# Two order tables joined at the first MoE matmul, the first units' attention reading whole copies of their keys

## The chip, the cores and the metric

The kernel runs on one core of a Trainium2 chip. The metric is the time of the device in microseconds; three executions of the kernel before give a median of 778.26 us (778.2 to 780.05). The trace is of one execution more, which took 779.34 us. TensorE (PE in the rows) multiplies, VectorE (DVE), ScalarE (ACT) and GpSimd (POOL) do the element-wise work, and SyncE (SP) issues most transfers. Each runs its own queue of instructions in order.

## What is computed

A block-sparse attention over 4 batches, 8 heads, 768 positions of 64 numbers, in blocks of 32, is followed by a MoE-like layer with one gated product.

```python
B, H, S, D = q.shape                      # 4, 8, 768, 64
scores = scale * np.matmul(q, k.transpose(0, 1, 3, 2))
mask = np.abs(blk_i - blk_j) <= 1
mask = mask | (blk_i == 0) | (blk_j == 0) | (blk_i == n_blocks - 1) | (blk_j == n_blocks - 1)
for qb in range(n_blocks):
    for kb in sampled_blocks[qb]:         # three sampled blocks for each block
        mask[qb * 32:(qb + 1) * 32, kb * 32:(kb + 1) * 32] = True
scores = np.where(mask, scores, -1000000000.0)
attn = softmax(scores)
x = (attn @ v).transpose(0, 2, 1, 3).reshape(B * S, H * D)
h = x @ w_in                              # (3072, 512) @ (512, 2048)
g = h * np.clip(h + 3.0, 0.0, 6.0) / 6.0
return g @ w_out                          # (3072, 2048) @ (2048, 512)
```

## The kernel before

**Units, chunks, weights.** A unit is one batch and four blocks of queries (a "quad" each). The string `SEQ` (line 39) gives their order; units 0, 1 and 2 are groups 1, 2 and 3 of batch 0, so blocks 3 to 14. Three units make a chunk of 384 columns, and the layer runs by chunk in 16 steps `m0`, `m1` and so on: `h` (line 657) is twelve matmuls out of one weight tile, `ga` and `gb` apply the gate, `gh` and `gl` split it into a high and a low part, `o` multiplies it with the output weight of three units. Weights `w0` to `w31` are input and output tiles in turn. They come as 64-bit words and are put together by `size`, `sign`, `low` and `bits`, then split by `hi` and `lo`.

**A unit's keys.** A query block attends to eight slots: the three blocks near it, block 0 and block 23 (the ends), and three chosen by a table. For batch 0 all keys are loaded first into `KN`, in three parts of eight blocks (`keys` of the constants, line 325). For units 0 to 2 only the three chosen blocks are copied on the chip, into slots 5 to 7 of a ring of six buffers `KR` (`chosen`, line 394; the block's number is read into registers by `registers`, line 383, sixteen at a time); near and ends are read from `KN` directly. So `keys_of` (line 443) hands out three places, and `s` (line 474) makes three matmuls of 96, 64 and 96 columns for each of four quads, two halves of the partitions and two heads: 48 for half a unit. Later units load their keys from memory into the ring (`keys` of an item, line 399), five blocks at a slot's first use in a batch and three after that, and three more by number; their `s` is one matmul of 256 columns for each, 16 for a half.

**The chain of a unit.** `s` (scores), `r_` (VectorE: bias and minimum), `e` (ScalarE: exponential), `t` (transposes), `c` (copy out of PSUM), `a` (values), `n_` (division), `x` (transposes), `xh` and `xl` (high and low part of the layer's input). `m0 h` needs those of units 0 to 2. Values come by `values` (SP) and, for the chosen blocks, by `gather` (an indirect transfer that GpSimd issues, with the addresses of the tile `rows`).

**The order.** The string `SCORE` (line 43) is an order written out: `u1 s0` is unit 1's first half of scores, `w4 low.d` the weight 4's `low` on VectorE (`a` ScalarE, `p` GpSimd, `s` SyncE). The loop at the end of `fused_kernel` issues the operations in that order, and `Ordered` (line 232, the operations' line in the profile is 242) keeps each engine's in it. What stands earlier in an engine's queue holds up what stands behind it.

Of the kernel before, what the change touches and what calls it, by code (L numbers as in the profile page):

```python
# [49 lines left out]
chosen0.d; u1 s0; u0 e03 e13; u1 gather0.p; u0 d t01; u1 r_00; w4 size; u0 t10; u1 gather2.p; w4 low.d; u1 e00; u0 t11 c01.d c10.a; u1 s1 r_01; u2  # L50
gather2.p; u0 c11.a; w4 sign; u1 e01 r_02; w1 size; u2 gather1.p; w4 bits; u1 t00; u3 q; u1 e02 r_10 c00.a r_03; u2 gather0.p; u1 e10; w5 load5; u1
r_11 e03; u2 chosen3.d; u0 a; u1 e11; u2 gather3.p; u1 r_12; u2 chosen2.a; w1 low.d; u1 r_13 e12; w1 sign; w0 size; u2 s0; u3 gather2.p; u0 n_; u1
e13; u3 keys1; w0 low.a; w1 bits; w2 size; u1 d; u0 x; u2 r_00; w1 hi.p; w2 low.a; u1 t01; u2 r_01; u1 t10; u2 e00; u3 gather0.p; w2 sign; w8 load8;
u1 t11 c01.a; u2 r_02 s1; u1 c10.a; w1 lo.d; w7 load7; u1 c11.a; u2 r_03 e02; w3 low.p; u2 e01; u1 a; u2 r_10; w6 low.p; u2 e03 r_11 e10; u3
gather1.p; w2 bits; u0 xh; u2 e11 r_12; u0 xl; w3 size; w10 load1; u2 t00; u4 gather1.p; u1 n_; u2 e12 t01 c00.a r_13 t10; u4 gather0.p; u2 c01.a; w0
sign; u1 x; u2 e13; w3 sign; u1 xh; u2 t11 d c10.a; u1 xl; u2 c11.a; w0 bits; w6 size; u2 a; w5 size; w3 bits; w9 load0; u3 keys2 gather3.p; w0 hi.a;
w6 sign; w2 hi.a; w0 lo.d; w3 hi.a; u2 n_; w5 low.a; w2 lo.p; w8 low.a; u2 x; w12 load3; w6 bits; w8 size; u2 xh; w3 lo.d; w7 size; u2 xl; w11 load2;
w7 low.a; w8 sign; m0 h; w7 sign; w10 low.a; u3 values2; w8 bits; w10 size; w7 bits; m1 h; w4 hi.a; w10 sign; m0 ga; w4 lo.d; w9 size; u3 values1; m0
gb; w9 low.a sign; m2 h; m0 gh.a; u3 keys0; w5 sign; m1 ga; m0 gl.d; w6 hi.a; m1 gb; m0 o0; w6 lo.d; w8 hi.a; m1 gh.a; w5 bits; m3 h; u3 values3; m2
ga; m1 gl.d; w12 size; m2 gb; w13 load4; w11 low.p; w12 low.a; u3 values0; w11 size; w8 lo.d; m0 o1; w16 load7; m3 ga; w10 bits; m1 o0; m3 gb; w10  # L60
hi.a; m0 o2; u3 keys3; w9 bits; m1 o1; m2 gh.a; w10 lo.d; m4 h; m2 gl.d; w13 size; w11 sign; w13 low.a; w14 load5; w12 sign; u4 q; w17 load8; m1 o2;
w11 bits; m4 ga; w15 load6; w16 size; m5 h; w12 bits; m3 gh.a; m4 gb; w5 hi.p; w7 hi.a; w12 hi.a; w13 sign; u4 keys0; w16 low.a; u3 s0; w5 lo.d; w12
lo.d; m2 o0; w14 low.a; u3 r_00; m3 gl.p; m6 h; w14 size; u3 r_01; u4 values0; w13 bits; u3 e00; w18 load0; u3 e01 r_02; w7 lo.p; m5 ga; u3 r_03 s1
e02; w22 load4; m5 gb; u3 e03; w14 sign; w20 load2; m2 o1; w15 size; u3 r_10; w15 low.p; w17 size; m3 o0; u3 r_11 e10; w14 bits; u4 keys2; m2 o2; u3
e11 r_12; w17 low.p; m3 o1; w14 hi.a; u3 r_13; m4 gh.a; u3 t00; w14 lo.d; w9 hi.a; u3 t01 t10; m4 gl.d; u3 e13; u5 q; m3 o2; u3 c01.a; w9 lo.d; u4
values1; u3 c10.a; m7 h; w21 load3; w15 sign; m6 ga; w16 sign; w11 hi.a; u3 e12; m6 gb; w19 load1; m5 gh.p; u3 c00.a; m4 o0; w16 bits; w18 size; u4
keys3; u3 t11; m5 gl.d; w16 hi.a; m4 o1; w15 bits; m7 ga; u3 c11.a; m4 o2; w16 lo.d; w20 size; m7 gb; u3 a; w11 lo.p; w13 hi.a; w20 low.a; w13 lo.d;
w22 size; m8 h; u4 keys1; u3 d; u4 gather3.p; w19 size; w17 sign; w21 low.a; u3 n_; w18 low.p; w22 low.a; m5 o0; w17 bits; u4 gather2.p; w19 low.a; u5
keys0; u3 x; m6 gh.d; w21 size; m5 o1; w20 sign; u5 gather0.p; u3 xh; m6 gl.d; m5 o2; u3 xl; m8 ga; u5 gather1.p; m6 o0; w20 bits; m7 gh.a; w15 hi.a;
m6 o1; m8 gb; u4 values2; m7 gl.d; u4 values3 s0; w25 load2; w15 lo.d; m6 o2; w18 sign; u5 values1; u4 r_00; m7 o0; m8 gh.a; w18 bits; u4 e00; u5  # L70
keys1; m7 o1; u4 r_01; w17 hi.a; m8 gl.d; u4 e01; m7 o2; u4 r_02; w17 lo.p; w18 hi.a; u4 r_03 t00 e02 s1 e03; w22 sign; w23 load0; u5 values0; u4
c00.a; w18 lo.d; m8 o0; w20 hi.a; u4 r_10; w25 low.p size; u4 t01 r_11; u6 q; m8 o1; u4 e10; w20 lo.d; u4 e11; m9 h; u4 r_12 c01.a; w22 bits; u4 e12;
u5 keys2; u4 r_13; w21 sign; u4 e13 t10; w23 size; w19 sign; m10 h; w22 hi.a; u4 d; w26 load4; u4 c10.a; w19 bits; m9 ga; w22 lo.d; w24 load1; w19
hi.a; u4 t11; m9 gb; m8 o2; m10 ga; w23 low.p; u4 c11.a; m10 gb; m11 h; m9 gh.a; w19 lo.d; m10 gh.a; w23 sign; u5 keys3; m9 gl.d; u4 a; w23 bits; m11
ga; w26 size; w21 bits; w26 low.a; m11 gb; w27 load0; w21 hi.p; m9 o0; u5 values2; u4 n_; w24 size; u5 values3 gather2.p; w24 low.a; w21 lo.d; u4 x;
m9 o1; m10 gl.d; u4 xh; u5 gather3.p; w24 sign; m10 o0; u4 xl; m9 o2; u6 gather2.p keys3; w24 bits; u5 s0; m11 gh.a; w25 sign; w23 hi.a; u6 gather3.p;
m10 o1; m11 gl.d; w24 hi.a; u5 r_00; w27 size; m10 o2; w24 lo.d; u5 e00; w28 load1; u5 r_01; w27 low.p; m12 h; u5 e01 r_02; w23 lo.d; u5 e02 r_03; w25
bits; u5 e03 s1; m12 ga; w26 sign; w29 load2; u6 keys2; m11 o0; m12 gb; w25 hi.p; u5 r_10; m12 gh.a; u5 t00; w25 lo.d; m11 o1; u5 e10 r_11 c00.a; m12
gl.p; m11 o2; w28 size; u5 r_12; u6 values3; w26 bits; u5 e11 t01; u6 values2; m12 o0; u5 e12 r_13; w28 low.p; w26 hi.a; u5 t10; w27 sign; u5 e13; m12
o1; u5 c01.a; w26 lo.d; u5 t11 c10.a; m12 o2; w27 bits; u5 c11.a; m13 h; w29 size; u5 d; w30 load0; w27 hi.a; w28 sign; w27 lo.d; u5 a; w28 bits; m13  # L80
ga; w29 low.d; w28 hi.a; w31 load1; m13 gb; w28 lo.d; u6 s0; m13 gh.a; u8 gather0.p; u6 values4; w30 low.a; u5 n_; m14 h; m13 gl.d; w30 size; u6 r_00;
# [696 lines left out]
```

## Time and profile before

| | us |
|---|---|
| median of three executions | 778.26 |
| lowest, highest | 778.2, 780.05 |
| the profiled execution, whole | 779.34 |
| its span, first to last instruction | 777.6 |
| busy in the span: TensorE | 754.0 |
| VectorE | 520.9 |
| ScalarE | 406.5 |
| GpSimd | 187.3 |
| start of `m0 h` in the span | 58.46 |

The profile gives busy time by engine and by slice, the groups of instructions with their mean time, and instructions in order of time with the idle time ahead of them and what ended it. Times in the rows count from the start of the span. A busy TensorE need not be at its peak, and matmul ends are modelled. The names of tiles are those of the code: `kn` and `kr` are `KN` and the ring, `att`, `h` and `out` are PSUM banks that the first units share.

### The profile page before, as it was taken

How to read it: one execution, taken by the hardware profiler on the slowest of the kernel's cores; microseconds unless marked ns; L12 is line 12 of the kernel's file. 1: busy time of each engine (PE TensorE's matmuls, PEld its weight loads, DVE VectorE, ACT ScalarE, POOL GpSimd, SP SyncE). 2: the span in 40 equal slices, each digit the busy share in tenths (PEclk: the TensorE clock that was granted, in tenths of full speed). 3: DMA queues.
4: the chain of work that ended last, by engine and by line, in shares of the span. 5: the costliest groups of instructions: out<-in, count | busy, mean ns of one | idle time of the engine just before them, and what ended most of it. 6: DMA issues, size and time to landing. Idle time of an engine off the chain costs nothing.

```text
span 777.6 us, 22739 instructions
## 1 busy us (share of the span) xinstructions
PE 754.0 (97%) x9078; PEld 649.8 (84%) x9078; DVE 520.9 (67%) x1304; ACT 406.5 (52%) x996; POOL 187.3 (24%) x200
## 2 busy tenths in 40 slices
PE   5789999999999999999999999999999999999996
PEld 5679887888888888898888888888888898889985
DVE  2568988955565665565656666767777677676763
ACT  2677977847555656455656553343543522452122
POOL 4531434141332221102123004222013511300110
PEclk9999999999999999999999999999999999999999
DMA  9949997660464673147245517464145670201001
GB/s 325 392 171 305 297 301 262 195 211 15 151 184 118 180 234 117 42 122 215 70 143 179 168 43 225 170 185 145 62 148 141 206 255 2 83 3 41 0 1 41
DMA packets 79687, 119.53 MB, mean 154 GB/s; under 512 B 10018, under 2 KB 45990, under 8 KB 79582
## 3 DMA queue, kind: packets, MB, share of 16 engines
q1 hardware_dynamic: 72674, 96.18, 38.6%
q0 software_dynamic: 6640, 21.76, 8.9%
q8 instruction: 72, 1.18, 0.6%
q14 instruction: 33, 0.27, 0.1%
...
HBM read 111.75 MB, written 6.29 MB: 152 GB/s over the span
## 4 chain that ended last, share of the span: by engine, by line
PE 89%; DVE 1%; DMA 0%; issue 0%; ACT 0%; ACTq 0%
PE out L242 35%; PE h L242 33%; PE att L242 21%; DMA out_dram<-ot 0%; DVE wout L242 0%; DVE wlo_in L242 0%; DVE wlo_out L242 0%; ACT ot L242 0%; DVE g L242 0%; DVE win L242 0%; ACTq L242 0%
## 5 line engine op out<-in xcount | busy, mean ns | idle before, releaser
L242 PE MATMUL h<-x,whi_in 128*128 128x384 f32 x1024 | 265.1, 339 | 1.7 <-ACT x L242 1.4
L242 PEld LDWEIGHTS h<-x,whi_in 128*128 128x128 f32 x1024 | 186.9, 189 | 12.3 <-ACT x L242 1.6
L242 PE MATMUL h<-x,wlo_in 128*128 128x384 f32 x512 | 172.9, 338 | 0.3 <-DVE wlo_in L242 0.3
L242 PE MATMUL out<-whi_out,ghi 128*128 128x512 f32 x384 | 162.2, 422 | 0.0
L242 ACT ACTIVATE p<-p,m 128x256 f32<-128x256 f32 x224 | 112.6, 504 | 83.8 <-DVE m L242 82.9
L242 PE MATMUL out<-whi_out,glo 128*128 128x512 f32 x384 | 151.6, 395 | 0.0
L242 PE MATMUL out<-wlo_out,ghi 128*128 128x512 f32 x384 | 151.1, 394 | 0.0
L242 ACT ACTIVATE g<-h,half_b 128x384 f32<-128x384 f32 x128 | 73.0, 580 | 149.2 <-PE h L242 131.6
L242 POOL DMA_INDIRECT vr<-vB,rows x77 | 76.9, 999 | 167.9 <-PE att L242 145.7
L242 DVE SCALAR_TENSOR_TENSOR g<-g,h 128x384 f32<-128x384 f32 x128 | 69.7, 551 | 57.8 <-ACT g L242 57.2
L242 PEld LDWEIGHTS h<-x,wlo_in 128*128 128x128 f32 x512 | 96.5, 188 | 0.6 <-DVE wlo_in L242 0.6
L242 PEld LDWEIGHTS out<-whi_out,ghi 128*128 128x128 f32 x384 | 72.2, 188 | 22.3 <-issue 12.3
L242 DVE TENSOR_TENSOR wlo_out<-wout,whi_out 128x512 fp32r<-128x512 f32 x106 | 76.1, 718 | 21.9 <-ACT whi_out L242 18.9
L242 DVE TENSOR_TENSOR wlo_in<-win,whi_in 128x512 fp32r<-128x512 f32 x107 | 75.2, 704 | 21.0 <-ACT whi_in L242 18.4
L242 DVE CUSTOM_DVE_ANT_1 p<-att,bias 128x256 f32<-128x256 f32 x176 | 68.6, 419 | 25.8 <-PE att L242 25.5
L242 PEld LDWEIGHTS out<-whi_out,glo 128*128 128x128 f32 x384 | 72.1, 188 | 16.3
L242 PEld LDWEIGHTS out<-wlo_out,ghi 128*128 128x128 f32 x384 | 72.5, 189 | 7.7
L242 DVE TENSOR_TENSOR glo<-g,ghi 128x384 fp32r<-128x384 f32 x114 | 67.9, 596 | 14.2 <-ACT ghi L242 12.0
L242 POOL TENSOR_TENSOR wlo_in<-win,whi_in 128x512 fp32r<-128x512 f32 x21 | 27.8, 1322 | 160.1 <-DVE whi_in L242 105.5
L242 ACT CAST ghi<-g 128x384 fp32r<-128x384 f32 x94 | 47.9, 512 | 32.1 <-PE out L242 29.4
L242 ACT COPY pt<-att 128x512 f32<-128x512 f32 x89 | 51.0, 586 | 24.6 <-PE att L242 23.7
L242 PE MATMUL att<-kr,q 64*32 64x256 f32 (+1 forms) x1280 | 59.7, 376 | 0.7 <-issue 0.7
...
## 6 DMA issues: line engine op xcount, KB each, us to landing
...
kr<-kS SPq DMA_DIRECT2D x52, 192.0 KB
vr<-vS SPq DMA_DIRECT2D x49, 192.0 KB
vr<-vS SPq DMA_DIRECT2D x33, 256.0 KB
kr<-kS SPq DMA_DIRECT2D x24, 320.0 KB
kn<-kN SPq DMA_DIRECT2D x12, 512.0 KB
q<-qT SPq DMA_DIRECT2D x24, 256.0 KB
vr<-vB SPq DMA_DIRECT2D x24, 256.0 KB
```

What stands on the lines that cost most here:

```text
L242: self.last = tc.keep_in_program_order(op(*a, **k)).ins
```

## The change

`SCORE` is new up to `m0 h`: 245 operations where there were 206. From `m0 h` on it is the same list of operations in the same order, without three that now stand ahead: `u3 values1`, `u3 keys0`, `w5 sign`. The new part names new operations. `near` copies a block's three near blocks from `KN` into slots 0 to 2, `ends` the two end blocks into slots 3 and 4, for units 0 to 2; all their slots are then in the ring and `s` is 16 matmuls for a half. `ends` runs once for each of the six buffers, and `holds_k` remembers it, so the later loads of these slots fetch three blocks and not five. `numbers` reads three registers for one item ahead of its copies. The small tables come in three loads instead of six, the constants 0.5 and -0.499 are passed as numbers, `warm` runs one exponential early, and `third` loads a part of `KN` (in the order 2, 0, 1).

```diff
-k0 load keys0; u0 q values1 values0 values2 values3; k0 clamp folding number flag; u0 chosen2.a; u1 q; u0 chosen0.p; k0 place; u1 values1 values0; u0
+k0 lp lc third2 lt third0 li third1 warm; u0 q; k0 clamp; u0 numbers2.p numbers1.a numbers3.d numbers0.a; u1 numbers0.a numbers1.p numbers3.d; u2
...
-        def load(self):
+        def lp(self):
             dma.dma_start(out=picked, in_=picks)
-            self.spr = p_tile().rearrange("p i k -> p (i k)")[:NB, :len(GROUPS) * P]
-            for to, src in ((turned, sampled_t), (place, placing), (samp, sampled), (cands, cand), (self.spr, spread), (ident, ident_d)):
-                act.dma_start(out=to, in_=src)
+
+        def lc(self):
+            t = p_tile().rearrange("p i k -> p (i k)")[:NB, :cand.shape[1]]
+            self.samp, self.cands, self.spr = t[:, :NR].bitcast(I32), t[:, NR:NR + 15], t[:, NR + 15:]
+            act.dma_start(out=t.bitcast(I32), in_=cand)
+
+        def lt(self):
+            act.dma_start(out=turning, in_=sampled_t)
+
+        def li(self):
+            act.dma_start(out=ident, in_=ident_d)
...
+        def third(self, i):
+            n = NB // 3
+            dma.dma_start(out=KN[:, n * i:n * (i + 1)].rearrange("p n h k -> p (n h k)"), in_=kN[0, :, n * P * i:n * P * (i + 1)])
+
+        def warm(self):
+            act.activation(out=warm, in_=nobias[:, :1], func=AF.Exp)
...
-            held = self.unit.held
+            o, n, at = 16 * self.unit.g, 16, 4 * self.quad
+            held = self.unit.held if eng is dma else self.held
+            if eng is not dma:
+                o, n, at = o + at, NR, 0
...
+        def near(self, eng):
+            self.has_near = True
+            copy(eng, self.K[:, :3], KN[:, self.blk - 1:self.blk + 2])
+
+        def ends(self, eng):
+            holds_k[self.kn] = self.unit.b
+            copy(eng, self.K[:, 3:5], KN[:, ::NB - 1])
...
-            return [(slice(3 * BLK), KN[rows_, item.blk - 1:item.blk + 2, hp]), (slice(3 * BLK, 5 * BLK), KN[rows_, ::NB - 1, hp]),
-                    (slice(5 * BLK, KEYS), item.K[rows_, 5:, hp])]
+            at, places = 0, []
+            if not item.has_near:
+                at = 3
+                places.append((slice(at * BLK), KN[rows_, item.blk - 1:item.blk + 2, hp]))
+            if holds_k.get(item.kn) != self.b:
+                places.append((slice(at * BLK, 5 * BLK), KN[rows_, ::NB - 1, hp]))
+                at = 5
+            return places + [(slice(at * BLK, KEYS), item.K[rows_, at:, hp])]
...
-                act.activation(out=to, in_=src, func=AF.Identity, scale=2.0 ** -29, bias=low_b)
+                act.activation(out=to, in_=src, func=AF.Identity, scale=2.0 ** -29, bias=LOW)
...
-            act.activation(out=self.g, in_=self.ps, func=AF.Relu, bias=half_b, scale=1.0 / 6.0)
+            act.activation(out=self.g, in_=self.ps, func=AF.Relu, bias=0.5, scale=1.0 / 6.0)
```

TensorE's queue at its start, before (`h` and `att` are the two PSUM banks of unit 0's first scores, `flags` and `place` belong to the tables):

```order
L242 MATMUL att<-turned_f,place 128x24
L242 MATMUL out_269<-flags,p 128x8 x6
L242 MATMUL h<-kn,q 32x96
L242 MATMUL h<-kn,q 32x64
L242 MATMUL h<-kr_73,q 32x96
L242 MATMUL att<-kn,q 32x96
L242 MATMUL att<-kn,q 32x64
L242 MATMUL att<-kr_73,q 32x96
```

and the same place after the change:

```order
L244 MATMUL att<-flags,p 128x8 x6
L244 MATMUL out_257<-turned_f,turned 128x24
L244 MATMUL h<-kr_73,q 32x256
L244 MATMUL att<-kr_73,q 32x256
L244 MATMUL h<-kr_74,q 32x256
L244 MATMUL att<-kr_74,q 32x256
```

Three pieces of a quad have become one, out of the ring alone, and the two small products ahead have changed places. The whole queue has 4352 entries where it had 4544.

ScalarE's queue from the last table loads to its first key copies, before (an entry ISA works out an address, `kr_75` is the buffer of unit 0's third item):

```order
L242 DMA samp<-sampled 24x3
L242 DMA cands<-cand 24x15
L242 DMA p<-spread 24x768
L242 DMA ident<-ident 128x128
L389 TENSOR_LOAD picked
L242 ISA
L242 ACT_TABLE_LOAD
L242 COPY kr_75<-kn 128x128
```

and after (128x256 is `ends`, 128x384 is `near`):

```order
L244 DMA p<-cand 24x786
L244 DMA turned<-sampled_t 4x152
L244 DMA ident<-ident 128x128
L244 ACT_TABLE_LOAD
L244 ACTIVATE warm<-nobias 128x1
L405 TENSOR_LOAD picked x5
L244 COPY kr_76<-kn 128x256
L244 COPY kr_73<-kn 128x384
L244 COPY kr_74<-kn 128x256
```

The copies that need no register now stand ahead of those that do, and the table load ahead of the wait for the keys.

GpSimd's queue at the end of unit 0's gathers, before (`vr_` is a buffer of values; `wout` and `win` serve as six more of them):

```order
L242 DMA vr_80<-vB,rows 128x512
L242 DMA vr_82<-vB,rows 128x512
L242 DMA vr_84<-vB,rows 128x512
L242 ISA
L242 COPY kr_73<-kn 128x128
```

and after:

```order
L244 DMA vr_79<-vB,rows 128x512
L244 DMA vr_82<-vB,rows 128x512
L244 DMA wout<-vB,rows 128x512
L244 ISA
L244 COPY kr_73<-kn 128x128
```

Behind unit 0's last gather (`vr_82`) stood one of unit 1 (`vr_84`); now it is one of unit 2 (`wout`), and unit 1's four come last.

## Rows read from the trace of the kernel before

**Rows 1.** The page: TensorE's busy time, and its tenths in 40 slices.
```profile
PE 754.0 (97%) x9078; PEld 649.8 (84%) x9078; DVE 520.9 (67%) x1304; ACT 406.5 (52%) x996; POOL 187.3 (24%) x200
...
PE   5789999999999999999999999999999999999996
```

**Rows 2.** Stretches: length, busy PE, PEld, DVE, ACT, POOL, granted clock, DMA share, GB/s.
```profile
0.00:11.20 11.20, 3.21 (x14) 3.12 (x14) 2.95 (x19) 2.58 (x7) 1.54 (x13) 1.00 0.81 276
11.20:34.80 23.60, 20.81 (x533) 19.32 (x533) 10.96 (x50) 13.30 (x45) 14.61 (x23) 1.00 1.03 393
34.80:47.30 12.50, 10.57 (x214) 9.77 (x208) 4.29 (x15) 5.70 (x16) 4.81 (x6) 0.86 0.71 269
47.30:58.46 11.16, 7.46 (x283) 6.42 (x281) 10.32 (x24) 10.68 (x25) 4.58 (x4) 1.00 0.46 141
58.46:64.60 6.14, 5.85 (x23) 5.60 (x24) 5.08 (x9) 4.45 (x8) 0.00 (x0) 0.72 1.00 295
64.60:777.60 713.00, 706.12 (x8023) 605.56 (x8021) 487.34 (x1190) 369.76 (x899) 161.76 (x155) 1.00 0.45 141
```

**Rows 3.** TensorE in order of time: start, length, operation, idle before.
```profile
8.58 2.72 PE L242 MATMUL out<-flags,p 24*128 24x8 f32 x12 [3.88 <-DVE flags L242]
11.23 0.74 PE L242 MATMUL h<-kn,q 64*32 64x96 f32 x4
...
16.01 0.27 PE L242 MATMUL out<-kn,q 64*32 64x96 f32 x1
...
19.50 0.66 PE L242 MATMUL att<-ident,p 128*128 128x128 f32 x4
...
56.41 0.66 PE L242 MATMUL out<-ident,xs 128*128 128x128 f32 x4 [1.89 <-DVE xs L242]
58.46 0.44 PE L242 MATMUL h<-x,whi_in 128*128 128x384 f32 x1 [1.39 <-ACT x L242]
...
77.48 1.09 PE L242 MATMUL att<-kr,q 64*32 64x256 f32 x32
```

**Rows 4.** TensorE's groups to 58.4 us: count, busy, mean ns, idle before.
```profile
L242 PE MATMUL out<-kn,q 64*32 64x64 f32 x80 | 11.5, 224 | 1.9 <-issue 1.9
...
L242 PE MATMUL out<-vr,pt 128*32 128x64 f32 x128 | 2.2, 220 | 2.1 <-issue 2.1
```

**Rows 5.** ScalarE in order of time.
```profile
8.55 1.29 ACT L242 COPY kr<-kn 128x128 f32 x6 [0.52 <-DMA kn<-kN]
16.75 0.51 ACT L242 ACTIVATE p<-p,m 128x256 f32<-128x256 f32 x1 [6.91 <-DVE m L242]
...
56.59 0.79 ACT L242 ACTIVATE wout<-wout,low_b 128x512 int32<-128x512 uint32 x1
57.26 0.68 ACT L242 ACTIVATE win<-wout 128x512 f32<-128x512 f32 x1
57.81 0.59 ACT L242 CAST x<-out 128x512 fp32r<-128x512 f32 x1
...
63.07 0.58 ACT L242 ACTIVATE g<-h,half_b 128x384 f32<-128x384 f32 x1
```

**Rows 6.** ScalarE's groups to 58.4 us.
```profile
L242 ACT ACTIVATE p<-p,m 128x256 f32<-128x256 f32 x24 | 12.1, 507 | 14.5 <-DVE m L242 14.5
...
L242 ACT COPY pt<-att 128x512 f32<-128x512 f32 x5 | 3.0, 591 | 3.8 <-PE att L242 3.8
```

**Rows 7.** GpSimd in order of time: the first and the twelfth gather.
```profile
13.86 1.13 POOL L242 DMA_INDIRECT vr<-vB,rows  x1 [0.32 <-issue]
...
28.80 0.94 POOL L242 DMA_INDIRECT wout<-vB,rows  x1 [0.31 <-issue]
```

**Rows 8.** DMA issues: tile, queue, count, size of one.
```profile
kr<-kS SPq DMA_DIRECT2D x52, 192.0 KB
...
vr<-vS SPq DMA_DIRECT2D x33, 256.0 KB
kr<-kS SPq DMA_DIRECT2D x24, 320.0 KB
kn<-kN SPq DMA_DIRECT2D x12, 512.0 KB
```

More of the change, by code (lines that the diff above doesn't have):

```diff
@@ L50 @@
[L50 to L81, printed above, removed]
@@ new lines @@
+gather0.p; u0 a; u1 e01 r_02; u3 keys1; u1 r_10 e02; u2 near3.d; u1 gather3.p e10 r_03; u2 near2.d; u1 e03 t00 r_11 gather2.p t01; u0 n_; u3 q; w2
+low.a; u1 r_12 e11; u0 x; u2 chosen3.p; u1 c01.d e12 t10 r_13; u2 chosen2.p; u0 xh; u1 c00.d c10.a gather1.p; u2 s0; u0 xl; u1 e13; w0 size low.d; w4
+load4; u1 gather0.p; w2 size; u1 t11 d; w3 load3; u2 s1 r_00; u1 c11.a; w2 sign; u2 e00; u3 gather1.p; u2 r_01; w1 low.a; w0 sign; w6 load6; u2 e01;
+u3 gather3.p; u2 r_02; u3 keys0; w1 size; u2 t00 r_10 e02 r_03; u3 gather2.p; u2 e10; w1 sign; u2 c00.a r_11 e03; u3 gather0.p; w1 bits; w5 load5; u2
@@ new lines @@
+e11 r_12; u1 a; w1 hi.a; w2 bits; u2 e12 r_13; k0 folding; w7 load7; w4 low.a; u2 e13; w1 lo.d; w4 size; u2 t01; u4 gather0.p; u1 n_; u2 t10 c01.a d
+t11 c10.a; u4 gather1.p; w4 sign; w8 load8; u1 x; u2 c11.a; w0 bits; u1 xh; u2 a; w3 low.a; w4 bits; w0 hi.a; u1 xl; w2 hi.a; w0 lo.d; w3 size; w2
+lo.d; w9 load0; w6 size; u3 keys2; w3 sign; w6 low.a sign; u2 n_; w5 low.a; w6 bits; u2 x; u3 values1; w5 size; w3 bits; u2 xh; w10 load1; w5 sign; w3
+hi.a; u2 xl; w7 size; w12 load3; w3 lo.d; w7 low.a; w8 low.a size; w11 load2; w8 sign; m0 h; w7 sign; w10 low.a; u3 values2; w8 bits; w10 size; w7
@@ new lines @@
+keys0; w16 low.a; u3 s0; w5 lo.d; w12 lo.d; m2 o0; w14 low.a; u3 r_00; m3 gl.p; m6 h; w14 size; u3 r_01; u4 values0; w13 bits; u3 e00; w18 load0; u3
+e01 r_02; w7 lo.p; m5 ga; u3 r_03 s1 e02; w22 load4; m5 gb; u3 e03; w14 sign; w20 load2; m2 o1; w15 size; u3 r_10; w15 low.p; w17 size; m3 o0; u3 r_11
+e10; w14 bits; u4 keys2; m2 o2; u3 e11 r_12; w17 low.p; m3 o1; w14 hi.a; u3 r_13; m4 gh.a; u3 t00; w14 lo.d; w9 hi.a; u3 t01 t10; m4 gl.d; u3 e13; u5
+q; m3 o2; u3 c01.a; w9 lo.d; u4 values1; u3 c10.a; m7 h; w21 load3; w15 sign; m6 ga; w16 sign; w11 hi.a; u3 e12; m6 gb; w19 load1; m5 gh.p; u3 c00.a;
@@ new lines @@
+m4 o0; w16 bits; w18 size; u4 keys3; u3 t11; m5 gl.d; w16 hi.a; m4 o1; w15 bits; m7 ga; u3 c11.a; m4 o2; w16 lo.d; w20 size; m7 gb; u3 a; w11 lo.p;
+w13 hi.a; w20 low.a; w13 lo.d; w22 size; m8 h; u4 keys1; u3 d; u4 gather3.p; w19 size; w17 sign; w21 low.a; u3 n_; w18 low.p; w22 low.a; m5 o0; w17
+bits; u4 gather2.p; w19 low.a; u5 keys0; u3 x; m6 gh.d; w21 size; m5 o1; w20 sign; u5 gather0.p; u3 xh; m6 gl.d; m5 o2; u3 xl; m8 ga; u5 gather1.p; m6
+o0; w20 bits; m7 gh.a; w15 hi.a; m6 o1; m8 gb; u4 values2; m7 gl.d; u4 values3 s0; w25 load2; w15 lo.d; m6 o2; w18 sign; u5 values1; u4 r_00; m7 o0;
@@ L479, in s @@
             for j in range(2):
+                todo = []
                 for q in range(4):
```

347 lines of the change are left out of this document (184 added, 163 removed).

## The prediction

> **What bounds the kernel now.** I read the page first. TensorE is busy 97% of the span and nine tenths or more of every slice but the first three and the last [rows 1]. So there are two kinds of time: a head of about 58 us before the first MoE matmul (`m0 h`), and a body in which TensorE is full. The stretches say the same [rows 2]: from 64.6 us to the end TensorE is busy 706.12 of 713.00 us, so an order change there could give at most 7 us; from 0 to 58.46 us it is busy 42.04 of 58.46. The diff leaves the order after `m0 h` as it was, but for three operations that move ahead of the joint (`u3 values1`, `u3 keys0`, `w5 sign`). The question is therefore when `m0 h` can start, and whether the body can follow at once.
>
> The head is set by TensorE itself, and this is the point that the busy share hides. A half of a unit's scores (`s`) is 48 small matmuls here, 16 times near, ends and chosen. Unit 0's second half starts at 16.01 and the first transposes follow at 19.50: 3.45 us [rows 3]. In the body the same half, 16 pieces of 256 keys out of one buffer, takes 1.09 us at 77.48 [rows 3]. Six halves stand before `m0 h`; they fill most of the 20.81 busy us of the stretch from 11.2 to 34.8. Two waits of 2.1 and 1.9 us inside the streams have no releaser that the profile shows [rows 4]; both stop a stream halfway. I take them for instructions that arrive late, and leave them out of the sum. The end of the head is a chain: unit 2's values, `n_`, a wait of 1.89 us, `x`, a wait of 1.39 us for `xh`, then `m0 h` at 58.46 [rows 3]. Transfers are full to 34.8 us (393 GB/s at a share of 1.03), and then have slack: 0.71 and 0.46 [rows 2].
>
> **The change part by part.**
>
> *Scores from one buffer.* All six halves lose 32 of 48 pieces. At the full clock that is 6 x (3.45 - 1.09) = 14.2 us of TensorE work gone from its own critical stretch; at half clock a new half costs 2.2 us. The engine starts slow: unit 0's first half took 4.78 us (11.23 to 16.01 [rows 3]).
>
> *The price: more key copies.* Near (384 columns) and ends (256) are now copied. ScalarE's copies of 128 columns cost 1.29 / 6 = 0.22 us apiece [rows 5], one of 512 about 0.5 in a row (its own duration is 0.591 [rows 6]), so by interpolation 0.30 for ends, 0.40 for near, 0.65 for a chosen trio. ScalarE gets 4 ends, 6 nears and 5 trios before unit 2's scores: 1.2 + 2.4 + 3.25 = 6.8 us, where it did four trios before. GpSimd and VectorE take the rest; they have room (4.81 and 4.29 us busy in 12.5 us [rows 2]).
>
> *The start.* Before, the first scores waited behind `spread` (8.58 [rows 3]) until 11.23, since the candidates' table came late in a row of six small loads. Now one load brings it and is issued first. The bound moves to the keys. ScalarE's first copy, which needs all three thirds, waited for them until 8.55 [rows 5]; ends and most nears need only two, which by size are in at some 6.2 us (an estimate: two thirds of the way from a first issue near 1.2 to 8.55). Four ends and two nears end at about 8.2, the two trios of unit 0 run from 8.5 to 9.8. So `u0 s0` starts at about 9.8 (no earlier than 8.5, no later than the old 11.2) and its first exponential, a half of 2.2 us and 0.7 later, at 12.7 instead of 16.75 [rows 5].
>
> *What becomes late next: ScalarE.* I add up its list to unit 2's `xh`: 24 exponentials at 12.1 / 24 = 0.5 [rows 6], 12 us; six copies of transposed scores at 0.5, 3 us; keys 6.8; and on weights six `low` at 0.67 (56.59 to 57.26), seven `size` at 0.55 (57.26 to 57.81) [rows 5], three `hi` and three `xh` at about 0.5: 10.9. Together 32.7. From 6.2 us on that ends at 38.9 if it never waits: the lower bound of `m0 h`. It does wait: 2.1 us from its copies to the first exponential, 0.6 for the second half, 1.9 until unit 1's scores are in, about 3 for unit 0's `xh`, which in its queue stands ahead of unit 1's last exponential while TensorE still does `u0 a`, `u1 t00`, `t01` and `u0 x`. That is some 7.6, of which half assumes the half clock. So **`m0 h` at 46.5** (38.9 + 7.6), against 58.46: 12.0 us earlier. Twice these waits would give 54.1; that is the upper bound I keep.
>
> *Gathers.* Before, GpSimd issued unit 0's to 2's twelve from 13.86 to 28.80 [rows 7], 1.25 us apart with chosen copies between. Now the first goes out at about 10 and unit 2's stand ahead of unit 1's, so that the last is unit 1's, at about 27.5. Unit 1's values are wanted near 32 us. Before, the share falls to 0.71 after 34.8 [rows 2], some 5 us after the twelfth issue, so that backlog had drained by then; 4 us earlier it drains by 31 to 32. I cost this at nothing. If that cover were gone, `u1 a` would wait with `u2 t01` to `t11` behind it in TensorE's queue, one gather's spacing (1.25 us) per place.
>
> *SP's queue.* `u3 keys1` stands behind three weights and ahead of `w4`; it waits for unit 1's scores, now over at about 23 us, and w4, w3, w6 wait with it. The transfers ahead of it are not through by then, so no engine of the 16 goes idle. The first use of a ring slot no longer fetches ends: six loads of 192 instead of 320 KB [rows 8], 0.79 MB or 2.0 us at 393 GB/s.
>
> *Table load, constants as numbers, folding later.* ScalarE's table load stood in its wait for the keys and now runs earlier still; no matmul of the head reads the folded matrix. I cost them at nothing, since the key loads hide them; uncovered, a GpSimd step of 0.3 to 0.5 us would be late for a gather.
>
> *Can the transfers follow?* `m0 ga` in ScalarE's queue stands behind `w3 hi`, w7, w8, w10 and `w4 hi`: 4.9 us, so at 51.4; it ran at 63.07 [rows 5], 11.7 us later. Its queue needs w10 landed by 49.6. By the order, ahead of w10's end lie keys 1.57, four q 1.05, values and gathers of three units 6.29, six gathers more 1.57, eleven weights 5.77 (0.524 each), unit 3's keys 1.18, the rest 0.34: 17.8 MB (a third of the keys, and so a weight, which is as large, from 512.0 KB [rows 8]). From about 2 us at 0.39 MB/us: 47.6. So 2.0 us to spare. A second way to the same place: the idle transfer time of before is 12.5 x 0.32 / 1.03 + 11.16 x 0.57 / 1.03 = 10.1 us [rows 2], and 2.0 us of bytes are gone: 12.1 us by which the head may shrink before transfers bind. The forecast uses just that. A shift above some 14 to 17 us is not to be had, whatever the engines do.
>
> *Sum.* The profiled execution took 779.34 us (span 777.6); 12 off gives 767.3. Against the median of the runs, 778.26, which I take as the base: **766.3 us**.
>
> *A rule that speaks against it.* TensorE fell to half clock twice (a mean of 0.86 in 34.8 to 47.3, of 0.72 in 58.46 to 64.6 [rows 2]); ahead of it lay a pause of 1.9 us, and two of 1.89 and 1.39 close together [rows 3, 4]; after the one of 2.1 [rows 4] it held (1.00 to 34.8). The new head has shorter bursts and more such pauses. The Trainium skill (TensorE: Matmul & The Clock Gate, section on HAM oscillation) says that bursts separated by waits can each start over at the slow clock. The trace agrees in kind, with two falls in 65 us; by the rule at its full strength the time would be that of the third rival, by the rows at their present rate that of the forecast.
>
> **The rivals.**
>
> *The chain has fewer waits.* If TensorE keeps the full clock and ScalarE waits 3 us, `m0 h` starts at 41.9; then w10 holds `m0 ga` until 47.6 + 1.8 = 49.4, a gain of 13.7, and with transfers at their best some 17: **761 to 764**. For it: slack on VectorE. Against: the byte sum.
>
> *The gain is eaten at the joint.* Waits twice as long (`m0 h` at 54.1, gain 4.4), or loads late after the joint: from 58.46 the share is already 1.00 at 295 GB/s [rows 2], not 393. If the last 4 MB ahead of `w10` move at 295, it lands 3.4 us later, 1.4 us past the spare time, and each of the next weights adds a little: a gain of 4 to 8, **770 to 774**.
>
> *Slower: the slow clock takes all of it.* At half rate throughout, the head's TensorE work grows by 6 x 1.09 (scores), 12 x 0.6 (transposes, one set at 19.50 [rows 3]), 3 x 2.2 (values [rows 4]) and 1.8 (three `x`): 22.1 us. About 5 are in the forecast. With the other 17.1 all on the chain `m0 h` would start at 63.6, and the kernel take **783.4**. It ends slower once more than 12.0 of the 17.1 lie on the chain. Against: `s` and `t` of unit 1 partly run beside ScalarE's exponentials.
>
> *It does not do what it says.* If some pieces still read three places, TensorE would not lose its work and the time would be that of before. The order shows 16 pieces of 256 in all six halves, so I give this next to nothing.
>
> **How the numbers follow.** Gain between 9 and 16 us: 0.66. More: 0.08. Between 2.3 and 9: 0.17. Within 0.3% (2.3 us, about what a measurement of this kernel can tell from no change): 0.03. Slower by more: 0.06. So faster 0.91, same 0.03, slower 0.06. The range goes from 761, a little past the transfers' bound, to 772.5, most of the eaten gain; the slower rival and the rest of the small gains stay outside.
>
> **What would show it.** In the profile after: halves of about 1.1 (or 2.2) us instead of 3.45; the first exponential near 12; ScalarE nearly full from 30 us to `m0 h`; `m0 h` near 46 and `m0 ga` near 51; a DMA share near 1 up to 60 us; and after `m0 ga` the same pieces with the same spacing. I am wrong if ScalarE has long waits before unit 2's exponentials, if TensorE's clock is half for most of the head, or if TensorE stands still after the joint for weights.

## The result, and the profile after

The kernel after takes 769.55 us (median of four runs, 768.52 to 771.27), the kernel before 778.53 (four runs, three of them those of its own table). The ratio is 0.9883, 95% interval 0.986 to 0.9906: 9.0 us or 1.2% faster. The forecast was 766.3, with a range of 761 to 772.5.

The profiled execution of after took 769.92 us with a span of 768.1 (before 779.34 and 777.6). The page of after, TensorE's row and its tenths, to be held against [rows 1]:

```profile
PE 742.4 (97%) x8694; PEld 632.6 (82%) x8694; DVE 525.8 (68%) x1308; ACT 398.7 (52%) x1009; POOL 185.9 (24%) x200
PE   6679999999999999999999999999999999999996
```

The stretches of after, columns as in [rows 2], cut at its own `m0 h`:

```profile
0.00:11.20 11.20, 4.55 (x46) 3.94 (x54) 3.91 (x22) 5.84 (x18) 4.38 (x16) 1.00 0.84 303
11.20:34.80 23.60, 19.45 (x443) 12.21 (x428) 19.26 (x71) 18.99 (x64) 18.29 (x27) 1.00 1.04 390
34.80:48.34 13.54, 5.89 (x179) 4.89 (x177) 9.14 (x19) 9.42 (x21) 2.31 (x2) 0.93 1.05 371
48.34:64.60 16.26, 16.19 (x72) 14.82 (x73) 14.18 (x24) 13.07 (x25) 1.32 (x2) 0.85 0.98 315
64.60:768.00 703.40, 696.35 (x7974) 596.69 (x7972) 479.26 (x1175) 351.35 (x884) 159.64 (x153) 1.00 0.44 136
```

Up to `m0 h` TensorE is busy 29.89 us (4.55 + 19.45 + 5.89) where it was busy 42.04; the head is shorter by 10.1 us. From 11.20 us on transfers are full up to `m0 h` (shares 1.04 and 1.05), where [rows 2] had 0.71 and 0.46 behind 34.80. From `m0 h` to the end the two kernels need the same time: 719.8 us after, 719.1 before.

TensorE in order of time, after (the rows that answer to [rows 3, 4]):

```profile
6.30 2.72 PE L244 MATMUL att<-flags,p 24*128 24x8 f32 x12 [6.30 <-DVE flags L244]
9.82 0.60 PE L244 MATMUL h<-kr,q 64*32 64x256 f32 x1 [0.34 <-POOL kr L244]
...
23.73 0.49 PE L244 MATMUL att<-vr,pt 128*32 128x64 f32 x20 [1.76 <-issue]
...
30.01 0.40 PE L244 MATMUL att<-kr,q 64*32 64x256 f32 x1 [0.74 <-issue]
...
33.30 0.25 PE L244 MATMUL out<-vr,pt 128*32 128x64 f32 x2 [1.17 <-DMA vr<-vB,rows]
...
37.88 0.22 PE L244 MATMUL out<-vr,pt 128*32 128x64 f32 x1 [3.06 <-issue]
...
44.87 0.24 PE L244 MATMUL att<-wout,pt 128*32 128x64 f32 x1 [3.10 <-issue]
46.55 1.12 PE L244 MATMUL out<-ident,xs 128*128 128x128 f32 x4 [0.81 <-DVE xs L244]
48.34 0.69 PE L244 MATMUL h<-x,whi_in 128*128 128x384 f32 x1 [0.68 <-ACT x L244]
...
68.07 1.09 PE L244 MATMUL att<-kr,q 64*32 64x256 f32 x32
```

`m0 h` starts at 48.34 instead of 58.46. The body's half of scores that stood at 77.48 [rows 3] stands at 68.07. And there are now four waits without a releaser, of 1.76, 0.74, 3.06 and 3.10 us: 8.7 in all, where [rows 4] had two of 2.1 and 1.9.

ScalarE, after (the rows that answer to [rows 5]), and its sum from 6.20 to `m0 h`:

```profile
12.33 0.51 ACT L244 ACTIVATE p<-p,m 128x256 f32<-128x256 f32 x1 [1.59 <-DVE m L244]
...
20.37 0.51 ACT L244 ACTIVATE p<-p,m 128x256 f32<-128x256 f32 x1 [1.35 <-DVE m L244]
...
23.94 0.71 ACT L244 ACTIVATE ot<-ot 128x512 int32<-128x512 uint32 x1 [0.99 <-DMA ot<-w_in]
...
26.16 0.51 ACT L244 ACTIVATE p<-p,m 128x256 f32<-128x256 f32 x1 [1.03 <-DVE m L244]
...
39.15 0.59 ACT L244 COPY pt<-h 128x512 f32<-128x512 f32 x1 [1.73 <-PE h L244]
...
44.92 0.70 ACT L244 ACTIVATE wout<-win 128x512 f32<-128x512 f32 x1
47.70 0.59 ACT L244 CAST x<-out 128x512 fp32r<-128x512 f32 x1 [2.08 <-PE out L244]
...
53.25 0.48 ACT L244 ACTIVATE g<-h 128x384 f32<-128x384 f32 x1
```

```profile
6.20:48.34 42.14, 29.90 (x651) 21.04 (x651) 30.39 (x99) 32.77 (x99) 24.63 (x39) 0.98 1.04 384
```

The fourth busy time is ScalarE's: 32.77 us of work in 42.14.

### The profile page after: what moved, and what is told of

It is laid out like the page before. It is cut to its first block, busy times and chain, and to the rows that moved or that the text cites. A ratio compares the mean times of both kernels' runs of the same rounds, so it can differ in the third digit from the quotient of the medians.

```text
span 768.1 us, 22001 instructions
## 1 busy us (share of the span) xinstructions
PE 742.4 (97%) x8694; PEld 632.6 (82%) x8694; DVE 525.8 (68%) x1308; ACT 398.7 (52%) x1009; POOL 185.9 (24%) x200
## 4 chain that ended last, share of the span: by engine, by line
PE 94%; issue 2%; DMA 1%; ACT 1%; POOL 1%; DVE 0%; DVEq 0%; POOLq 0%; ACTq 0%
PE out L244 37%; PE h L244 36%; PE att L244 22%; DMA vr<-vB,rows 1%; POOL kr L244 0%; ACT p L244 0%; DMA out_dram<-ot 0%; DVEq L405 0%; DMA picked<-picks 0%; ACT ot L244 0%; ACT kr L244 0%; DVE xs L244 0%; DVE flags L244 0%; DVE same L244 0%; ACT x L244 0%
## 5 line engine op out<-in xcount | busy, mean ns | idle before, releaser
L244 PEld LDWEIGHTS h<-x,whi_in 128*128 128x128 f32 x1024 | 187.0, 189 | 12.2 <-ACT x L244 1.1
L244 ACT ACTIVATE g<-h 128x384 f32<-128x384 f32 x128 | 61.6, 491 | 150.7 <-PE h L244 137.2
L244 DVE TENSOR_TENSOR glo<-g,ghi 128x384 fp32r<-128x384 f32 x114 | 67.7, 595 | 14.7 <-ACT ghi L244 12.9
L244 PE MATMUL att<-ident,p 128*128 128x128 f32 x420 | 61.0, 276 | 0.0
L244 PEld LDWEIGHTS att<-ident,p 128*128 128x128 f32 x420 | 51.1, 142 | 11.7 <-issue 1.2
```

The costliest lines, as they stand in the source:

```text
L244: self.last = tc.keep_in_program_order(op(*a, **k)).ins
```

## The experiments

The twelve runs fell on chips of two kinds. In the first comparison, and on the chip of the last two runs, the kernel before takes 778 to 780 us (the record does not say whether that is one chip or two); on three others it takes 800 to 802, and all times there are longer. Each numbered chip was used for one group of runs, so whether the difference belongs to the chip or to the hour stays open. So each run is told as its ratio to the before of its own chip, and its `m0 h` is compared only with traces from the same kind of chip. Each `m0 h` is from one trace, and the traces compared are often from different chips of a kind.

What follows speaks of **pieces** (16 large score matmuls for a half instead of 48), of the **order** (the new table), of **T1** (blocks of TensorE instructions arrive late and bind the head), and of **the list** (T2, L: ScalarE's work binds it).

### Is it the pieces or the order?

*Old reads.* After's order, but the scores read three places again.

```diff
         def near(self, eng):
-            self.has_near = True
-            copy(eng, self.K[:, :3], KN[:, self.blk - 1:self.blk + 2])
+            pass
         def ends(self, eng):
-            holds_k[self.kn] = self.unit.b
-            copy(eng, self.K[:, 3:5], KN[:, ::NB - 1])
+            pass
```

> The kernel after with its new order, but the scores of units 0 to 2 read near and ends out of KN again, 48 small matmuls for a half; the copies near and ends are not made, and the later loads of these slots fetch five blocks. Theory P (the 16 large pieces give the gain, by TensorE's time and by 768 fewer instructions in its stream): m0 h at 58 to 66 us, time 778 to 787. Rival O (the new order, the earlier tables and the earlier chosen copies give it): m0 h at 47 to 51, time 769 to 772. If both give half: m0 h near 53, time near 774.

*Old order.* Before's table and loads, with the copies inside `chosen`.

```diff
         def chosen(self, eng):
-            self.on_chip = True
+            self.on_chip = self.has_near = True
+            if holds_k.get(self.kn) != self.unit.b:
+                holds_k[self.kn] = self.unit.b
+                copy(eng, self.K[:, 3:5], KN[:, ::NB - 1])
+            copy(eng, self.K[:, :3], KN[:, self.blk - 1:self.blk + 2])
...
-            return [(slice(3 * BLK), KN[rows_, item.blk - 1:item.blk + 2, hp]), (slice(3 * BLK, 5 * BLK), KN[rows_, ::NB - 1, hp]),
-                    (slice(5 * BLK, KEYS), item.K[rows_, 5:, hp])]
+            return [(slice(KEYS), item.K[rows_, :, hp])]
```

> The kernel before with its old order and its six table loads, but the operation that copies the chosen blocks also copies near, and ends at a slot's first use, so that the scores of units 0 to 2 are 16 large pieces for a half. Theory P (the pieces give the gain): m0 h at 49 to 52, time 769 to 772, even though near is copied late in the row and the first scores start no earlier than before. Rival O (the order gives it, the copies in the old places cost as much as the pieces save): m0 h at 56 to 60, time 776 to 780.

Both fell on a chip of the slower kind (before 799.98). Old reads: 793.26, ratio 0.992 (0.9893 to 0.9946), `m0 h` at 60.61. Old order: 786.13, ratio 0.984 (0.9805 to 0.9876), `m0 h` at 56.00. The times expected were for a chip of the first kind, so only the ratios can be held against them: old reads keeps about half of the gain, where theory P left it none, and old order keeps all of it. After was not among those runs, so the second kernel was run again beside it.

> The kernel after, unchanged, beside the next three on the same chip, since the four runs before this one were on a chip on which the kernel before takes 800 us, not 778.5, and they had no run of after beside them. If a chip's slowness lies in late instructions alone (T1), the ratio to before on such a chip is at or below 0.98, since after has fewer instructions; if the slowness is the same for all work, the ratio is again 0.988. On a chip of the first kind: 0.988, m0 h at 48.3 within 0.5.

> The kernel before with its old order and loads, but with near and ends copied, so that the halves of scores are 16 large pieces; now beside the kernel after on one chip. Theory P (the pieces give the whole gain, and the new order gives none of its own because blocks of instructions bind the head): m0 h within 2 us of after's, and the same time within 0.3%. Rival O (the new order gives half or more of the gain): m0 h 5 us or more later than after's, and a time 4 to 8 us longer.

On one chip (before 801.77): after 788.25, ratio 0.984 (0.9822 to 0.9857); old order with the pieces 787.46, ratio 0.9824 (0.9797 to 0.9852). After's ratio lies between the two that were expected for it (0.98 and 0.988) and decides for neither. TensorE at `m0 h`, first after, then the old order:

```profile
53.42 1.41 PE L244 MATMUL h<-x,whi_in 128*128 128x384 f32 x2 [0.68 <-ACT x L244]
```

```profile
55.87 0.44 PE L242 MATMUL h<-x,whi_in 128*128 128x384 f32 x1 [1.40 <-ACT x L242]
```

So on this kind of chip theory P holds in the time: the pieces alone are worth 14 us, as much as the whole change, and the order adds 2.4 us at `m0 h` (a little over the 2 us that P allowed) that do not reach the end. By itself, with the old reads, the order is worth about 6.7. The two overlap. Whether the order adds more on a chip of the first kind was not run.

### What binds the new head?

*No gathers.* Units 0 to 2 get zeros from GpSimd where the gather stood.

```diff
         def gather(self, eng):
+            if self.unit.n < CHUNK:
+                pool.memset(self.V[:, 1], 0.0)
+                return
```

> The kernel after, but the twelve gathers of units 0 to 2 are left out and a GpSimd memset of zeros stands in their places (so the values of the ends and the chosen blocks are missing in the first three units). 3.1 MB fewer are moved before 40 us. Theory T1 (TensorE's instructions come in blocks of 256 over the same transfer engines, and a block comes late while these are full): the waits of TensorE without a releaser shrink from 8.7 us to under 4, and m0 h starts at 42 to 45 us. Rival T2 (ScalarE's list sets m0 h, and those waits lie beside it): the waits may shrink, but m0 h stays at 46.5 to 48.5.

*128 more instructions.*

```diff
-... third0 li third1 warm; u0 q; ...
+... third0 li third1 warm pad; u0 q; ...
...
+        def pad(self):
+            b = bank()
+            for i in range(32):
+                pe.matmul(b[:8, :8], lhsT=nobias, rhs=nobias, start=True, stop=True)
```

> The kernel after with 32 tiny matmuls of 8x8 (128 instructions of TensorE) ahead of everything else that TensorE does, in its idle start, where they cost nothing. Theory T1: the ends of the blocks of 256 instructions move by half a block, so every wait without a releaser moves to another place in the streams, 128 instructions earlier; the first blocks are crossed earlier, in slack, and m0 h starts 1 to 3 us earlier or later than 48.3, with the waits at other operations; time 766 to 771. Rival T2b (those waits belong to the operations at which they stand, the first values and the transposes): they stay where they are, and m0 h stays at 48.3 within 0.3.

*Half of the values.*

```diff
-                for c in range(2):
+                for c in range(1 if self.first else 2):
...
-                                  rhs=self.value(q).V[:, c, D * h:D * h + D], start=c == 0, stop=c == 1)
+                                  rhs=self.value(q).V[:, c, D * h:D * h + D], start=c == 0, stop=self.first or c == 1)
```

> The kernel after, but the values a of units 0 to 2 use only half of the keys (the second half of the contraction is left out, 64 matmuls of a unit instead of 128, so 768 fewer instructions of TensorE and some 3.3 us less of its work before m0 h, 6.6 us at half clock). Theory T1 (blocks of 256 instructions bind the head at some 7 us each): three blocks fewer, m0 h 5 us or more earlier than after's. Rival T2 (ScalarE's list binds; the values lie beside it): m0 h at most 2 us earlier.

*Late gathers.* The six gathers of units 3 and 4 taken out of `SCORE` ahead of `m0 h`, those of unit 3 put behind `m1 h`, those of unit 4 behind `m2 h`:

```diff
-u3 gather1.p; ... u3 gather3.p; ... u3 gather2.p; ... u3 gather0.p; ... u4 gather0.p; ... u4 gather1.p; ... m0 h; ... m1 h; ... m2 h;
+m0 h; ... m1 h; u3 gather1.p gather3.p gather2.p gather0.p; ... m2 h; u4 gather0.p gather1.p;
```

> The kernel after with the six gathers of units 3 and 4 moved from the 12 us ahead of m0 h to behind m0 h and m2 h: 1.57 MB less to move before m0 h, nothing left out. Theory T1 (transfers that are full hold up the blocks of instructions and the weights): the waits without a releaser after 30 us shrink, m0 h 1 to 3 us earlier, time 0 to 3 us shorter. Rival T2 (transfers ahead of m0 h don't hold it): m0 h unchanged within 0.5 us, time the same within 0.3%, or longer if the gathers delay unit 3's values or weights behind the joint.

*Lows on GpSimd*, alone and with the late gathers:

```diff
-w1 low.a; ... w4 low.a; ... w3 low.a; ... w6 low.a; ... w5 low.a; ... w7 low.a; w8 low.a; ... w10 low.a;
+w1 low.p; ... w4 low.p; ... w3 low.p; ... w6 low.p; ... w5 low.p; ... w7 low.p; w8 low.p; ... w10 low.p;
```

> The kernel after with eight operations low of weights (w1, w4, w3, w6, w5 ahead of m0 h, w7, w8, w10 behind it) moved from ScalarE to GpSimd, where one took 0.66 us against 0.67 and which stands idle for 13 us before m0 h. It takes five instructions, some 2.8 us by their spacing of 0.56, out of ScalarE's list before m0 h, and three, 1.7 us, out of the list before m0 ga. Theory L (ScalarE's list sets m0 h): m0 h 2 to 3 us earlier than in the kernel after on a chip of the same kind (48.3, or 53.4 where before takes 800 us), m0 ga 3 to 4.5 earlier, time 2 to 4 us shorter, a ratio to before of 0.979 to 0.982 on the slower chips and 0.984 to 0.986 on the other. Theory W (waits of TensorE, late instructions or held-up signals, set m0 h; the list lies beside them): m0 h unchanged within 0.7 us and the time within 0.3%.

> As the run before it, and the six gathers of units 3 and 4 moved behind m0 h and m2 h as well, so that GpSimd is free for the eight lows and 1.57 MB less are moved before m0 h. Theory L: the same as without the moved gathers, 2 to 3 us for m0 h. Theory W with the gathers as its cause: m0 h 1 to 3 us earlier than with the lows alone. If both count: 4 to 5 us, a ratio to before near 0.977 on the slower chips.

All six fell on chips of the slower kind. After there has `m0 h` at 53.42 and a ratio of 0.984.

| run | `m0 h` | ratio to before, interval |
|---|---|---|
| no gathers | 47.83 | one run, 781.97 against 799.98 |
| 128 more instructions | 53.59 | 0.9807 (0.978 to 0.9834) |
| half of the values | 56.15 | 0.9848 (0.9827 to 0.9869) |
| late gathers | 53.57 | 0.9826 (0.9806 to 0.9846) |
| lows on GpSimd | 54.65 | 0.984 (0.9797 to 0.9884) |
| lows on GpSimd, late gathers | 51.35 | 0.9802 (0.9753 to 0.9852) |

**TensorE's instructions.** With 768 of them fewer (half of the values) `m0 h` comes no earlier, so T1 as a bound falls on this kind of chip. TensorE's busy time to `m0 h` did not fall with them: it is 35.49 us where after has 34.74, at a granted clock of 0.82 where after has 0.87.

What T1 says of the waits themselves, the added instructions bear out. TensorE's records (matmuls and weight loads, the second and third count of a row) can be counted up to each wait. After on the first chip, cut inside the four waits, then after and the padded kernel on the slower kind:

```profile
0.00:22.50 22.50, 14.84 (x220) 10.02 (x221) 13.57 (x61) 14.55 (x52) 13.16 (x28) 1.00 0.94 347
22.50:29.60 7.10, 5.54 (x126) 3.76 (x125) 4.40 (x16) 5.08 (x14) 5.95 (x11) 1.00 1.04 385
29.60:36.00 6.40, 3.64 (x127) 2.37 (x128) 6.00 (x20) 6.09 (x20) 3.57 (x5) 1.00 1.04 397
36.00:43.00 7.00, 3.89 (x127) 3.46 (x126) 4.00 (x9) 5.27 (x12) 2.31 (x2) 1.00 1.04 390
```

```profile
0.00:47.50 47.50, 32.75 (x600) 20.86 (x600) 26.54 (x102) 29.15 (x92) 23.95 (x45) 0.89 0.93 340
```

```profile
0.00:28.90 28.90, 20.92 (x348) 13.25 (x349) 13.52 (x62) 15.39 (x54) 15.75 (x35) 0.88 0.95 348
28.90:47.20 18.30, 13.42 (x252) 9.52 (x251) 12.97 (x38) 13.07 (x37) 8.41 (x11) 0.81 0.90 319
...
30.14 0.27 PE L244 MATMUL att<-vr,pt 128*32 128x64 f32 x2 [1.56 <-issue]
```

On the first chip the waits come after 441, 692, 947 and 1200 records, 251 to 255 apart, which is a block of 256 less the few records that a trace lacks. The padded kernel has a wait of 1.56 us after 697 records, among the last values of unit 0, where after shows none on either kind of chip, and one of 0.62 at 47.50 after 1200; after on the slower kind has one of 0.69 at 47.87, also after 1200. So 128 instructions ahead leave these waits at the same count and at other operations, as T1 said and T2b denied. `m0 h` did not move by the 1 to 3 us that T1 gave (53.59 against 53.42). On these chips there are other waits without a releaser, near 15.7, 17.1 or 25.4 us, that stand at no such count.

**ScalarE's list.** Moving lows to GpSimd shortens it, and gives nothing by itself. The sums to `m0 h`, first after, then with the lows on GpSimd (the fourth busy time is ScalarE's):

```profile
6.20:53.42 47.22, 34.74 (x651) 22.28 (x651) 30.11 (x99) 32.55 (x99) 23.61 (x39) 0.87 0.96 348
```

```profile
6.20:54.65 48.45, 35.37 (x651) 22.51 (x651) 32.14 (x99) 30.20 (x94) 30.27 (x46) 0.87 0.94 339
```

The list got 2.4 us shorter and its waits 3.6 us longer (47.22 - 32.55 = 14.7, then 18.25). But the run does not clear the list, for it made VectorE slower. After, then the lows on GpSimd:

```profile
46.10 0.69 DVE L244 SCALAR_TENSOR_TENSOR win<-win,wraw 128x512 int32<-128x512 int32 x1
```

```profile
46.06 1.19 DVE L244 SCALAR_TENSOR_TENSOR win<-win,wraw 128x512 int32<-128x512 int32 x1
...
46.78 1.04 POOL L244 TENSOR_SCALAR wout<-wout 128x512 int32<-128x512 uint32 x1
```

Beside GpSimd's lows four of VectorE's operations from 46 to 52 us took 1.11 to 1.19 us instead of 0.69, and the lows up to 1.11 instead of 0.65. In both runs unit 2's `x` on TensorE waits for VectorE's `xs` (2.89 and 4.50 us); `xs` came 1.24 us later (52.13 against 50.89), which is all that `m0 h` lost. With the late gathers as well `m0 h` came 2.1 us earlier, what theory L expected of the lows alone, but that is one trace on another chip. So the list stays a suspect, and VectorE's queue is one that no run tested.

**The gathers.** Taking out those of units 0 to 2 moved `m0 h` by 5.6 us (one run). The first 2.2 us of it are at the first exponential, and the traces show how. After on such a chip, ScalarE and then TensorE in order of time:

```profile
14.78 0.51 ACT L244 ACTIVATE p<-p,m 128x256 f32<-128x256 f32 x1 [3.83 <-issue]
...
16.20 0.51 ACT L244 ACTIVATE p<-p,m 128x256 f32<-128x256 f32 x1 [0.83 <-issue]
```

```profile
15.71 0.59 PE L244 MATMUL h<-kr,q 64*32 64x256 f32 x2 [0.80 <-issue]
...
17.15 0.73 PE L244 MATMUL att<-ident,p 128*128 128x128 f32 x3 [0.45 <-issue]
```

Two engines at once go forward in steps of 1.4 us (14.78 to 16.20, 15.71 to 17.15) and wait for nothing that the profile shows. GpSimd issues its gathers in that time. Without them ScalarE reads:

```profile
12.55 0.51 ACT L244 ACTIVATE p<-p,m 128x256 f32<-128x256 f32 x1 [1.60 <-DVE m L244]
```

That is close to the time of the first kind of chip (12.33). Full transfers are not the cause of these steps: from 11.20 to 18.00 they are as full without the gathers. After, then no gathers:

```profile
11.20:18.00 6.80, 5.29 (x52) 1.98 (x36) 1.78 (x9) 1.83 (x6) 4.36 (x7) 0.95 1.05 388
18.00:24.00 6.00, 5.15 (x47) 3.16 (x49) 4.92 (x18) 4.87 (x20) 4.62 (x6) 0.50 1.04 396
```

```profile
11.20:18.00 6.80, 4.86 (x62) 2.46 (x46) 5.33 (x21) 5.14 (x20) 3.81 (x10) 1.00 1.06 395
```

ScalarE is busy 5.14 us there instead of 1.83. And the stops have a price of their own: behind them TensorE's granted clock is 0.50 from 18 to 24 us, its lower level of 1.2 GHz.

### The gathers on another queue

The twelve gathers of units 0 to 2 as plain transfers of SyncE, alone, then with the lows on GpSimd and the late gathers:

```diff
-u0 gather1.p; ... u0 gather2.p; ... u0 gather0.p; ... u0 gather3.p; ... u1 gather0.p;
+u0 gather1.s; ... u0 gather2.s; ... u0 gather0.s; ... u0 gather3.s; ... u1 gather0.s;
```

> The kernel after with the twelve gathers of units 0 to 2 issued by SyncE as four plain transfers of 64 KB each, by block number, at the same places in the order, where GpSimd issued one indirect transfer each; the same bytes arrive in the same buffers and nothing is left out. SyncE's queue gets 48 issues of some 0.45 us, 22 us, so its weights and keys start later. Theory S (on a chip where before takes 800 us, GpSimd's indirect transfers hold up the signals and instructions of the other engines): the waits of ScalarE and VectorE of 2 to 4 us at 11 to 17 us and at 22 to 32 us go, the first exponential is at 12.3 and not at 14.8, and m0 h at 47 to 50 instead of 53.4. Theory B (it is the bytes, full transfers, that hold them up): the waits stay, and m0 h is at 53 to 56. On a chip of the other kind, where these waits do not exist: m0 h at 47.5 to 50, by SyncE's longer queue if later than 48.3.

> As the run before it, and also the eight operations low on GpSimd and the six gathers of units 3 and 4 behind m0 h and m2 h, so that no indirect transfer is left ahead of m0 h. Theory S: m0 h at 45 to 47 and a ratio to before of 0.972 to 0.978 on the slower kind of chip. Theory B: m0 h at 51 to 54, ratio 0.980 to 0.984. On a chip of the other kind: m0 h at 45 to 47, and a time 1 to 3 us shorter than that of the kernel after, if the weights behind the joint are not late.

They fell on a chip of the first kind (before 780.09), and both are slower than before: 786.91, ratio 1.0084 (1.006 to 1.0109), and 786.39, ratio 1.0085 (1.0062 to 1.0107). `m0 h` came at 64.00 and 65.71. So they could not tell S from B, and the expectations for this kind of chip (47.5 to 50, and 45 to 47) were wrong by 14 and 19 us. SyncE and then TensorE in the first of them:

```profile
28.66 3.38 SPq L244 DMA_DIRECT2D win<-vB  x4
...
47.06 1.94 SPq L244 DMA_DIRECT2D vr<-vB  x4
```

```profile
51.64 0.48 PE L244 MATMUL out<-vr,pt 128*32 128x64 f32 x3 [13.41 <-DMA vr<-vB]
...
64.00 1.41 PE L244 MATMUL h<-x,whi_in 128*128 128x384 f32 x2 [0.67 <-ACT x L244]
```

A gather of GpSimd is one issue of 1 us; on SyncE it is four issues, 1.9 to 3.5 us. Unit 1's last one goes out at 47.06 where after issues its twelfth at 26.08, and TensorE stands 13.4 us for it. The queue had room in bytes, not in issues. In that trace TensorE has one wait without a releaser in the head, 1.04 us, where after has 8.7; from 22 to 47 us the transfers were at a share of about 0.7.

## Why the prediction was right, step by step

**Where the gain is made: right.** It is 10.1 us at `m0 h` (48.34 against 58.46), 9.8 at `m0 ga` (53.25 against 63.07), 9.4 at the body's half of scores, and 9.5 in the span. Little is eaten at the joint: 0.7 us between `m0 h` and the body's half. From 48.34 to 66 us no engine waits for a transfer, so the weight that was priced to land at 47.6 was not late. The second rival fell. So did the first: ScalarE waited more than the forecast's 7.6 us, not less.

**TensorE's work: right in kind.** The forecast took 14.2 us out of the head; the busy time fell by 12.2. The first half still starts slow: it takes 1.96 us (9.82 to 11.78) where the body's takes 1.09; the forecast had 2.2. The row of that stretch shows a granted clock of 1.00, so the slow pace is read off the matmuls alone.

**The start: right.** First scores at 9.82 (forecast 9.8), first exponential at 12.33 (forecast 12.7, before 16.75 [rows 5]).

**ScalarE's list: right.** The forecast was 32.7 us of work from 6.2 on; the trace has 32.77.

**Its waits: the term that was too small.** The forecast was 7.6; the trace has 9.37 (42.14 - 32.77). The difference, 1.8 us, is the whole error of `m0 h` (46.5 forecast, 48.34 measured). That it is so small is in part luck. The places that the forecast named (2.1, 0.6, 1.9 and 3) came to 4.0 at most: 1.59, none, 1.35 and 1.03. The other 5.4 it had not named: 1.73 at 39.15 and 2.08 at 47.70 for products of TensorE that late waits hold up, and 1.3 for weights that had not landed (0.99 at 23.94, 0.31 at 35.72). The step that failed is the sentence "I take them for instructions that arrive late, and leave them out of the sum". They did not stay at 4 us, they became 8.7. In after the instructions of TensorE come in packets of their own, one of 16 KB at a time. The queues of after from 35.40 to 36.60 us (packets, MB, share of 16 engines):

```profile
q1 hardware_dynamic: 63, 0.24, 50.1%
q0 software_dynamic: 68, 0.22, 48.6%
q8 instruction: 1, 0.02, 5.7%
```

This packet starts at 35.45, after TensorE has stopped at 34.82, and ends at 36.54; the wait of 3.06 ends at 37.88. The others end at 22.38, 28.64 and 43.53; the waits end at 23.73, 30.01 and 44.87, each 1.3 to 1.4 us behind. These four packets take 1.0 to 1.1 us each, so what makes one late is when it starts. In before the two waits that end at 33.69 and 38.95 stand 1.2 to 1.3 us behind packets that end at 32.39 and 37.71. The Trainium skill (Runtime: NRT & Kernel Launch, section Instruction fetch mechanics) says that instructions are refilled in blocks of 16 KiB, 256 of them, and that crossing from one to the next is mostly hidden. The trace agrees with the block. It does not agree with hidden: in this head four crossings cost 8.7 us of TensorE's time. Beyond 48 us after has one such wait, 0.71 us at 258. That the full transfers are what makes the packets late is argued and not shown: no run changed them alone, and without gathers one crossing still cost 1.94 us, at 23.47.

Not all of the 8.7 is on the path. ScalarE finishes its list at 45.6 and waits 2.08 us for unit 2's `x`, which the wait of 3.10 at 44.87 has put late. But VectorE, which makes `xs` for that product, waited less:

```profile
45.80 0.69 DVE L244 TENSOR_TENSOR xs<-att,m 128x512 f32<-128x512 f32 x1 [0.97 <-PE att L244]
```

Its queue was busy until 44.83, so without that one wait `m0 h` would come at most 0.97 us earlier, near 47.4 (an estimate); the rest of the 1.8 us lies in the waits before it. This is read off the trace; no run on that kind of chip tested it, and the runs on the other kind could not.

**Gathers at nothing: wrong, within its price.** TensorE waits 1.17 us at 33.30 for a gather of unit 1; the text had given 1.25 us per place if the cover were gone.

**The bytes: the second count was too high.** The second way to the transfers' bound took off all six key loads that no longer fetch ends, 2.0 us. In after only three of them are issued ahead of `m0 h` (20.86, 30.80 and 41.25), 0.39 MB or 1.0 us, so that way gives 11.1 us and not 12.1. The sum of the forecast does not use it.

**The clock: right on the first kind of chip, not on the other.** From 6.20 to 48.34 the granted clock is 0.98, so the third rival fell. It did fall behind the waits of 3.06 and 3.10, to 0.50 (1.2 GHz), but mostly behind `m0 h`, from 48.34 to 52.00. On the slower chips it is 0.87 over the same work, and 0.50 behind the stops. The rule of the Trainium skill (TensorE: Matmul & The Clock Gate, section on HAM oscillation) that the prediction weighed, bursts that start over at the slow clock behind waits, agrees with these traces in kind; on the chip of the prediction it stayed small.

**Not foreseen at all:** that the pieces would be enough. The forecast counts the earlier start as part of the gain. On the slower kind of chip the old order with the pieces is as fast, and the early start is lost there to the stops: the first exponential comes at 14.78, and at 15.91 with the old order.

What stays open: what in a gather holds the other engines up where before takes 800 us and not where it takes 778; what makes the blocks late; how much of the new head is ScalarE's list and how much VectorE's queue; and whether lows on GpSimd with late gathers beat after. They lie at 784.97 where after, on another chip of the kind, has 788.25, but their ratios overlap.
